# Gate and up on the centred h, with the layer norm's scale multiplied in as their rows leave PSUM

## The chip, the cores and the metric

One core of a Trainium2 chip. The metric is device time in microseconds (us) of one execution. Besides the time, each run lists the span that the profile sees of each execution and the mean clock granted to TensorE over it (1.0 is full). All comparisons are of runs of state fast, the mark for a run within 1.5% of its kernel's fastest.

In the profile's lines PE is TensorE (PEld its weight loads), DVE is VectorE, ACT is ScalarE, DMA a transfer. A load is whole, or has landed, when the last of its 16 semaphore increments is recorded. An eviction is the copy of a product out of PSUM, where the matmuls leave it. The chain of waits is the work that ended last, followed back from its end.

## The reference, cut to what matters

Decode step of one block: layer norm, attention over a cache, layer norm, gated feed-forward, two batch rows.

```python
def _layernorm(x, axis=-1, eps=1e-5):
    m = jnp.mean(x, axis=axis, keepdims=True)
    v = jnp.var(x, axis=axis, keepdims=True)
    return (x - m) / jnp.sqrt(v + eps)
# ... attention A, D = 640, F = 1536, B = 2
def _B_ref(x, w_gate, w_up, w_down):
    return (_gelu(x @ w_gate) * (x @ w_up)) @ w_down
h = x + _A_ref(_layernorm(x, axis=-1), A_k_cache, A_v_cache, A_wq, A_wo)
h2 = h + _B_ref(_layernorm(h, axis=-1), B_w_gate, B_w_up, B_w_down)
```

The scale 1/sqrt(v + eps) is one number per batch row, so it may be multiplied in after the gate and up products, ahead of the gelu.

## The kernel before

The program records operations per engine in order; `R`, `W`, `X` name what an operation reads, writes, and which PSUM bank it uses, and waits follow from them. The tail of the kernel, with cuts marked:

```python
# loads, in this order at the end of one queue: ... wo(2), wo(3), gate, up in 2 parts, down in 4 parts
WDC = ((0, 6), (6, 9), (9, 11), (11, 12))
# ...
def layernorm(src, src_toks, banks, dst, dst_tok, total=None):
    # ... total None: as for x
    else:
        pe(total, R=["rs", "bsel"], X=["m2"])
    dve(lambda e: e.tensor_copy(mean[:, :], m2[:, 16:18]), W=["mean"], X=["m2"])
    dve(tt(dT[:, 0, :, :], src, mean..., ALU.subtract), ...)
    dve(tt(dT[:, 1, :, :], dT[:, 0, :, :], dT[:, 0, :, :], ALU.mult), ...)
    dve(lambda e: e.tensor_reduce(out=ls[:, 1, :], in_=dT[:, 1, :, :]..., op=ALU.add), ...)
    pe(lambda e: e.matmul(m2[:, 20:22], lhsT=onesd[:, :], rhs=ls[:, 1, :], start=True, stop=True), ...)
    act(... ACT.Ln, bias=eps ...); act(... ACT.Exp, scale=-0.5 ...)
    dve(tt(dst, dT[:, 0] ..., lt[:, 1, :] ..., ALU.mult), R=["dT0", "lt1"], W=[dst_tok])
# ...
oproj(3)                        # the last attention weights; h and its row sums
h_columns()                     # h by columns, 20 small fp32 matmuls
layernorm(...)                  # writes hnT, bf16
ffn_in(sps, "s", "wg", ...)     # gate: 20 matmuls, hnT stationary, 384 columns moving
dve(lambda e: e.tensor_copy(grow[0:98, 0:384], sps[0:98, 0:384]), W=["sm"], X=["s"])
# ... transposes of the gate rows, gelu on VectorE and ScalarE
ffn_in(ops_, "o", "wu", WUC)    # up: 20 matmuls in two parts
act(... urow[0:98, :], in_=ops_[0:98, 0:384], func=ACT.Copy ...)
# ... transposes of the up rows, product uT
for i, (f0, f1) in enumerate(WDC):   # down: 48 matmuls, each part waits for its own load
    wd, wtoks = where["wd", i]
    # ...
dve(... yrow <- m1 ...); out is stored
```

## Time and profile before

| | before |
|---|---|
| time, 3 runs | 293.97, 294.00, 294.27 us |
| the profiled execution | 294.86 us, span 292.8, mean clock 0.827 |
| read from HBM | 122.29 MB |

### The profile page before, as it was taken

What the parts mean: (1) busy time and instruction counts of PE and PEld (TensorE: products, weight loads), DVE (VectorE), ACT (ScalarE), POOL (GpSimd) and SP (SyncE); (2) the same over time, 40 slices, a digit from 0 to 9 for tenths busy, and PEclk for the clock granted to TensorE, in tenths of its full rate; (3) what the DMA queues carried; (4) which work ended last, traced back from release to release, by engine and by line L of the source; (5) the groups of instructions that cost most, each with busy time, mean ns of one, the idle gap of its engine ahead of it and who ended that gap; (6) DMA issues with size and microseconds to landing.
All of it is one profiled execution on the core that took longest, in us unless ns stands there. A gap on an engine that the chain in (4) does not pass through costs nothing.

```text
span 292.8 us, 5063 instructions
## 1 busy us (share of the span) xinstructions
PE 197.3 (67%) x2141; PEld 153.7 (52%) x2141; DVE 128.3 (44%) x310; ACT 96.2 (33%) x120; POOL 8.6 (3%) x36
## 2 busy tenths in 40 slices
PE   2450869848677298849495697668696869676575
PEld 1440436718475295628282675366666666653342
DVE  5950075713447055526255255316365425352222
ACT  2150116623442143616152245234343434430000
POOL 4000020000000000000000000000000000000000
PEclk9995679995979579988879599959797969797655
DMA  7998999999999999999999999999999999999993
GB/s 272 468 488 358 435 426 437 432 425 430 425 419 436 430 430 428 430 430 430 433 421 437 430 430 430 430 430 430 430 430 430 433 430 430 430 430 433 419 410 126
DMA packets 6363, 122.44 MB, mean 418 GB/s; under 512 B 719, under 2 KB 849, under 8 KB 1361
## 3 DMA queue, kind: packets, MB, share of 16 engines
q1 hardware_dynamic: 6336, 122.29, 97.8%
q8 instruction: 7, 0.11, 0.2%
q14 instruction: 4, 0.02, 0.0%
q10 hardware_dynamic: 16, 0.01, 0.0%
HBM read 122.29 MB, written 0.00 MB: 418 GB/s over the span
## 4 chain that ended last, share of the span: by engine, by line
DMA 71%; PE 24%; SPq 1%; DVE 1%; issue 1%; ACT 0%
DMA ring<-in_A_k_cache_dram 52%; PE tps L553 16%; DMA ring<-in_A_wq_dram 10%; DMA ring<-in_A_wo_dram 9%; PE tps L574 2%; SPq L343 1%; PE m L706 1%; PE ops L655 1%; PE m L829 1%; PE sps L783 1%; PE ops L783 1%; PE m L688 1%; PE tps L792 1%; PE m L725 0%; DVE ering L404 0%
## 5 line engine op out<-in xcount | busy, mean ns | idle before, releaser
L553 PE MATMUL tps<-identf,ring 128*128 128x128 f32 x768 | 115.6, 319 | 43.7 <-DMA ring<-in_A_k_cache_dram 42.3
L553 PEld LDWEIGHTS tps<-identf,ring 128*128 128x128 f32 x768 | 106.8, 168 | 46.8 <-DMA ring<-in_A_k_cache_dram 43.9
L562 ACT ACTIVATE ktr<-tps 128x1024 bf16<-128x1024 bf16 x80 | 79.4, 1023 | 83.5 <-PE tps L553 83.5
L565 DVE COPY ktr<-tps 128x1024 bf16<-128x1024 bf16 x112 | 74.1, 688 | 70.6 <-PE tps L553 69.8
L630 ACT ACTIVATE eexp<-sm,nm 128x512 bf16<-128x512 f32 x16 | 11.5, 722 | 64.5 <-DVE nm L628 64.5
L655 PE MATMUL ops<-ring,ering 128*32 128x384 bf16 x512 | 24.6, 336 | 4.9 <-DMA ring<-in_A_v_cache_dram 4.8
L611 PE MATMUL sps<-ktr,rq 128*16 128x512 bf16 x384 | 26.0, 405 | 1.1 <-POOL rq L404 1.1
L619 DVE CUSTOM_DVE_ANT_1 sm<-sps,mska 128x512 f32<-128x512 f32 x16 | 11.1, 692 | 35.2 <-PE sps L611 35.2
L655 PEld LDWEIGHTS ops<-ring,ering 128*32 128x32 bf16 x512 | 12.6, 98 | 13.3 <-DMA ring<-in_A_v_cache_dram 6.2
L611 PEld LDWEIGHTS sps<-ktr,rq 128*16 128x16 bf16 x384 | 9.5, 90 | 12.0 <-issue 2.1
L626 PEld LDWEIGHTS m<-mrhs,pm 128*128 128x128 bf16 x16 | 1.5, 96 | 22.9 <-DVE mrhs L400 22.9
L574 PE MATMUL tps<-ring,xnT 128*32 128x384 bf16 x80 | 5.8, 478 | 10.8 <-DMA ring<-in_A_wq_dram 10.8
L626 PE MATMUL m<-mrhs,pm 128*128 128x16 bf16 x16 | 2.9, 183 | 14.7 <-DVE mrhs L400 14.7
L404 POOL TENSOR_TENSOR rq<-qs,mask 128x96 bf16<-128x96 bf16 x16 | 5.6, 359 | 195.3 <-PE sps L611 161.3
L574 PEld LDWEIGHTS tps<-ring,xnT 128*32 128x32 bf16 x80 | 3.3, 138 | 13.2 <-issue 11.0
L597 DVE CAST qs<-ops 128x384 bf16<-128x384 f32 x1 | 0.6, 558 | 17.6 <-PE ops L592 17.6
L404 DVE TENSOR_TENSOR ering<-m,mask 128x256 bf16<-128x256 f32 x16 | 6.7, 420 | 3.4 <-PE m L639 3.4
L458 ACT ACTIVATE lt<-m,eps_t 128x2 f32<-128x2 f32 x2 | 0.5, 262 | 21.2 <-PE m L456 21.2
L706 PE MATMUL m<-ring,ot 128*2 128x320 bf16 x96 | 4.7, 340 | 2.4 <-DMA ring<-in_A_wo_dram 2.4
L581 ACT ACTIVATE qrow<-tps 128x768 bf16<-128x768 f32 x1 | 0.8, 810 | 15.6 <-PE tps L574 15.6
L639 PE MATMUL m<-sel,eexp 128*128 128x64 bf16 x64 | 5.0, 206 | 1.2 <-ACT eexp L630 1.2
L639 PEld LDWEIGHTS m<-sel,eexp 128*128 128x128 bf16 x64 | 4.8, 112 | 1.7 <-DVE nm L628 1.3
(116 smaller groups left out, 88.5 us busy)
## 6 DMA issues: line engine op xcount, KB each, us to landing
ring<-in_A_k_cache_dram SPq DMA_DIRECT2D x16, 3072.0 KB, 31.4
ring<-in_A_v_cache_dram SPq DMA_DIRECT2D x16, 3072.0 KB, 27.3
ring<-in_A_wq_dram SPq DMA_DIRECT2D x1, 7680.0 KB, 28.1
ring<-in_A_wo_dram SPq DMA_DIRECT2D x4, 1920.0 KB, 21.3
ring<-in_B_w_gate_dram SPq DMA_DIRECT2D x1, 1920.0 KB, 31.4
ring<-in_B_w_up_dram SPq DMA_DIRECT2D x1, 1536.0 KB, 24.7
ring<-in_B_w_down_dram SPq DMA_DIRECT2D x1, 960.0 KB, 27.2
ring<-in_B_w_down_dram SPq DMA_DIRECT2D x1, 480.0 KB, 27.9
```

The costliest lines, as they stand in the source:

```text
L404: return lambda e: e.tensor_tensor(out=out, in0=a, in1=b, op=op)
L553: ins = e.transpose(tps[bi][:, 128 * u:128 * (u + 1)], kv[:, off:off + 128], identf[:, :])
L562: act(lambda e, dst=dst, bv=bv: e.activation(out=dst, in_=bv, func=ACT.Copy), W=[("kt", n)], X=[("t", bi)])
L565: dve(lambda e, dst=dst, bv=bv: e.tensor_copy(dst, bv), W=[("kt", n)], X=[("t", bi)], cls=0)
L574: ins = e.matmul(tps[0][32 * r:32 * (r + 1), 0:384], lhsT=xnT[:, c, 32 * J:32 * (J + 1)], rhs=wq[:, c, 1536 * J + 384 * r:1536 * J + 384 * ...
L611: ins = e.matmul(sps[32 * ch:32 * ch + 16, :], lhsT=rq[:, g % 4, k, :], rhs=ktr[:, k // 2, 1024 * ch + k % 2:1024 * (ch + 1):2], start=(k ...
L619: dve(lambda e: e.tensor_tensor_reduce(out=sm[:, :].rearrange("p (u x) -> p u x", u=4), in0=sps[:, :].rearrange("p (u x) -> p u x", u=4), ...
L630: act(lambda e: e.activation(out=eexp[:, :], in_=sm[:, :], func=ACT.Exp, bias=nm[:, 0:1], scale=1.0, accum_out=zr[:, g % 4:g % 4 + 1]), R= ...
L639: ins = e.matmul(o, lhsT=eexp[:, 128 * u:128 * (u + 1)], rhs=sel64[:, :], start=True, stop=True)
L655: ins = e.matmul(ops_[32 * r:32 * (r + 1), 0:384], lhsT=ering[:, g % 4, t, :], rhs=vv[:, 384 * t:384 * (t + 1)], start=(g % 4 == 0 and t < 4),
L706: ins = e.matmul(m1[32 * r:32 * r + 2, 192:512], lhsT=ot[:, kk, :], rhs=wo[:, kk - k0, 320 * h:320 * (h + 1)], start=(kk == 1 or J < 2 and ...
L783: ins = e.matmul(bank[32 * r:32 * r + 2, 0:384], lhsT=hnT[:, c, :], rhs=cols[:, :, 3 * (r % 2):3 * (r % 2) + 3], start=(c == 0), stop=(c = ...
```

## The change

Its intent: take the norm's serial steps off the path between h and the gate. Four parts: the mean's matmul goes ahead of the column matmuls, into a bank of its own; gate and up take the centred h; square, sum, Ln and Exp run beside the gate, with the sum's matmul after eight of its 20; the scale is applied by the two evictions.

```diff
+        dve(lambda e: e.memset(lsx[:, :, :], 0.0), W=["lsx"])
 ...
+        pe(lambda e: e.matmul(tps[3][:, 0:2], lhsT=rs[0:98, :].to_broadcast([98, 128]), rhs=bsel[0:98, :], start=True, stop=True),
+           R=["rs", "bsel"], X=[("t", 3)])
         h_columns()
-        layernorm(m2[:, 32:42].rearrange("p (c b) -> p c b", b=B), [], ["m2"], hnT[:, :, :].unsqueeze(2), "hnT", ...)
+        dve(lambda e: e.tensor_copy(mean[:, :], tps[3][:, 0:2]), W=["mean"], X=[("t", 3)])
+        dve(tt(hnT[:, :, :], hc, mb, ALU.subtract), R=["mean"], W=["hnT"], X=["m2"])
+        dve(tt(dT[:, 0, :, :], hc, mb, ALU.subtract), R=["mean"], W=["dT0"], X=["m2"])
+        dve(tt(dsq[:, :, :, :], db, db, ALU.mult), R=["dT0"], W=["dsq"])
+        dve(lambda e: e.tensor_reduce(out=lsx[:, :, 0:B], in_=dsq[:, :, :, :], axis=AX.X, op=ALU.add), ...)
+        def row_scale():
+            pe(... matmul(tps[2][0:98, 0:1], lhsT=lsx ... [:, 0:98], rhs=onesd[:, 0:1] ...))
+            act(... lnv, ACT.Ln, bias=eps ...)
+            act(... rstd, ACT.Exp, scale=-0.5 ...)
 ...
-        ffn_in(sps, "s", "wg", ((0, NC5),))
-        dve(lambda e: e.tensor_copy(grow[0:98, 0:384], sps[0:98, 0:384]), W=["sm"], X=["s"])
+        ffn_in(sps, "s", "wg", ((0, 2),), ((0, NC5),))
+        row_scale()
+        ffn_in(sps, "s", "wg", ((2, NC5),), ((0, NC5),))
+        dve(ts(grow[0:98, 0:384], sps[0:98, 0:384], rstd[0:98, 0:1], ALU.mult), R=["rstd"], W=["sm"], X=["s"])
 ...
-        act(... func=ACT.Copy), W=[("osb", 0), ("osb", 1)], X=["o"])
+        act(... func=ACT.Identity, scale=rstd[0:98, 0:1]), R=["rstd"], W=[("osb", 0), ("osb", 1)], X=["o"])
```

The rewritten loop of `ffn_in` lets one load be used in two pieces.

## The prediction

> **What bounds the kernel now.** I read the page's rows over time first, for what the whole span is bound by, then the chain of waits, for its last piece, then the DMA issues, for when the last weights land.
>
> ```profile
> DMA  7998999999999999999999999999999999999993
> GB/s 272 468 488 358 435 426 437 432 425 430 425 419 436 430 430 428 430 430 430 433 421 437 430 430 430 430 430 430 430 430 430 433 430 430 430 430 433 419 410 126
> PEclk9995679995979579988879599959797969797655
> DMA 71%; PE 24%; SPq 1%; DVE 1%; issue 1%; ACT 0%
> ```
>
> The transfers are busy in every slice but the last, at 420 to 437 GB/s: 122.29 MB have to come in, and the change removes no byte. So only the end, after the stream has nearly run out, can get shorter. The chain from 275 us on is compute:
>
> ```profile
> 248.00 27.34 DMA ring<-in_A_wo_dram
> ...
> 277.85 1.30 PE m L725 x20
> 279.15 0.53 PE m L773 x2
> 279.68 0.02 issue
> 279.70 0.17 DVE mean L450
> ...
> 281.68 0.18 DVE hnT L404
> 281.86 0.04 issue
> 281.90 1.80 PE sps L783 x19
> 283.70 0.02 issue
> 283.72 0.57 DVE sm L808
> ...
> 288.46 1.81 PE m L829 x48
> 290.27 0.02 issue
> 290.29 0.33 DVE yrow L835
> ```
>
> Columns: start, duration, what. The last attention weights land at 275.34; then h, its columns (L725), the mean (L773), the layer norm, gate (first L783), its eviction (L808), up, down (L829), copy out. Between the mean's matmul (ends 279.68) and the gate (starts 281.90) lie 2.22 us of small serial steps.
>
> The trap is that the chain names only what released each step last. The same transfers still run beside it. The DMA issues, with the start of each issue, say when each weight is whole:
>
> ```profile
> ring<-in_B_w_gate_dram SPq DMA_DIRECT2D x1, 1920.0 KB, 31.4
> ring<-in_B_w_up_dram SPq DMA_DIRECT2D x1, 1536.0 KB, 24.7
> ring<-in_B_w_down_dram SPq DMA_DIRECT2D x1, 160.0 KB, 28.2
> ```
>
> Gate is issued at 248.47 and takes 31.4 us: whole at 279.87. The landing records give wu0 283.57, wu1 284.54, and the four down parts 286.88, 288.07, 288.86, 289.26. Against use: gate at 281.90 (2.03 us to spare), up at 285.10 (1.53 to spare), the first down part at 288.46 (1.58 to spare), but the last part, four matmuls that start at about 289.84 (290.27, less 0.34 for one matmul, less three spacings of 0.03), has only 0.58 us to spare. The busy share of the DMA engines agrees: 0.43 in 288.0 to 288.5, 0.13 in 288.5 to 289.0, then nothing. From 275.34 to 289.26 they bring gate, up and down, 5.90 MB, which is 424 GB/s: the stream is full and can't come sooner.
>
> **What the Trainium skill says.** "DMA: Bandwidth & Descriptors", section "Why a DMA increments its semaphore by 16 and not by 1": only the full count means that everything has landed. The trace agrees: of the last down part the first of 16 increments comes at 287.36 and the last at 289.26, so the late one counts. "TensorE: Matmul & The Clock Gate", Part 1: the tensor clock is full or half, by how busy TensorE was in windows of about 3.4 us. The trace has 0.50 in every window from 275 us on, so the tail's durations are those of the half clock; I keep them. "ScalarE: Activation LUTs", section "What ACT_TABLE_LOAD costs": each per-partition pointer operand adds about 93 ns to an ACTIVATE, and a switch of table set costs about 2.66 us. The changed program has the same single table load as the old one, at its start, so only the 93 ns count; no row of this trace shows them for this shape. "VectorE: DVE Perf Modes", section "Why PSUM operands drop a tier": an fp32 source in PSUM runs at the base rate whatever the operation, so the scaling eviction should last what the plain copy did (0.56 us for 384 columns).
>
> **The change part by part, on the clock of the trace of before.**
>
> 1. The mean's matmul (0.53 to 0.58) goes ahead of the column matmuls (1.30). TensorE is free at about 279.70 as before, but the mean's copy (0.17) now lies beside the column matmuls.
> 2. VectorE then makes the centred h in bf16: 279.70 to 279.88. Gone from between are copy, square, reduction, sum matmul (0.60), Ln (0.27), Exp (0.21) and the final multiply. The gate could start at 279.92. But its weights are whole only at 279.87, and a wait for a transfer is followed in this trace by 0.13 us (275.34 to 275.47) until TensorE starts. So 280.00: 1.90 sooner than 281.90.
> 3. Row scale. VectorE: centred fp32 (0.17), square of 40 columns and reduction of 40 (about 0.2 each, from 0.17 for 10 and 0.18 for 24 columns): ready at about 280.5. TensorE meets its new matmul after eight of the 20 gate matmuls, at 280.00 + 8 x 0.08 = 280.64, so it doesn't wait. The new fp32 matmul (two passes, 128x98 weights) is of the kind of the sum matmul removed, whose weight loads last 0.50 and whose matmuls 0.59; I charge 0.5 us, now inside the gate. Gate ends at 280.00 + 1.80 + 0.5 = 282.3. Ln and Exp (0.5 together) end at about 281.8, beside it.
> 4. Eviction with scale, 0.57: 282.9. Transposes 0.77 and gaps: 283.7. Up weights (283.57 + 0.13) are just there. Up 1.73: 285.45, its last part (284.54) in time.
> 5. Up's eviction on ScalarE 0.50 + 0.09, transposes 0.77, product 0.23, gaps 0.1: down can start at about 287.15, 1.3 us sooner than 288.46. That is the whole gain of compute: 1.98 of norm, less 0.08 of landing, 0.5 of row scale and 0.09 of ScalarE.
> 6. Down then runs into its own weights. 24 matmuls from 287.15 end at 287.9; 12 from 288.07 + 0.13 end at 288.6; 8 from 288.86 + 0.13 at 289.25; the last 4 from 289.26 + 0.13 = 289.39. Four matmuls at a spacing of 0.03 with 0.34 for the last end at 289.82. The copy out starts at 289.84 and not at 290.29: **0.45 us saved**. Of 1.3 us of compute, 0.85 turn into waits for the last down parts.
>
> At the start there is one more small memset on VectorE (lsx), before 13.3 us, delaying copies of the first keys slightly; those are done at 19.9 and the next work waits for the query weights, whole at 29.50, so it costs nothing. Sum: 294.0 - 0.45 = 293.55 us.
>
> **The rivals.**
>
> A. The landings don't bind, and all of the compute gain shows: 294.0 - 1.3 = 292.7. For it: the chain of waits of before has no transfer in it after 275.34. Against: the landing of the last part at 289.26 doesn't depend on compute, since its buffers were free and it was issued by 261.1; and it is 1.0 us before the old end of down.
>
> B. The row scale holds the gate up: VectorE's sums come late, or the fp32 matmul between two groups of gate matmuls drains the pipeline, at 1 us or more and not 0.5. Down has 0.87 us of slack (it may start at 289.39 - 44 x 0.031 = 288.0 without harm), so this costs nothing up to about 1.4 us in all; at 2 us the time would be back to about 294.1. Against it: the sum is ready about 0.15 us before TensorE comes to it.
>
> C. Gate or up wait longer for their own weights, since both are now consumed within about 0.15 us of landing. The landings are fixed by the stream, so this could eat tenths of the compute gain, all of it within the 0.87 us that down waits anyway: 293.55 again.
>
> D. The clock of the last windows changes with the denser work. At full clock the tail's matmuls halve, but they are hidden behind the landings except the last four and the first after 275.34: 0.2 us less, 293.3.
>
> **Range and chances.** The most that could be saved in any way I can see is about 2.2 us (0.7%), and a loss of 2% would take 5.9 us, over twice the whole of the norm. So within 2% it is: 0.985. The three runs of before lie 0.3 us apart, and the landing of the last part moves by tenths between executions; with A at about one in ten and B or a full cancelling at one in ten, the range is 293.0 to 294.0.
>
> **What would show it.** Right: in the profile after, gate starts about 280 with hnT as its releaser or the gate weights; the new matmul sits among the gate matmuls at about 0.5 us; down starts near 287.1 and is spread over about 2.7 us where it took 1.81, with TensorE's waits before it put down to the down weights; the chain of waits ends in the transfer of the down weights, then a few matmuls, then the copy at 1 us or less after 289.26. DMA rows unchanged. Wrong: down in one block of 1.8 us that ends before 289.3 (rival A, landings earlier than I read them), or a gate group that ends after 283.0 (B), or a landing of the last down part that moved by more than 0.3 us, which would mean that the change touches the stream after all.

## The result, and the profile after

The changed kernel took 294.07 us (median of 6, 293.96 to 294.18), the kernel before 294.20 in the same rounds (median of 6, 293.97 to 294.78): ratio 0.9994, 95% interval 0.9981 to 1.0006. A ratio here is the mean time of one kernel's fast runs over that of the other's of the same rounds, so not quite the ratio of the medians. The prediction, 293.55 within 293.0 to 294.0, is missed by 0.07 us at its upper end and by 0.5 at its centre. What is odd: the trace after looks as forecast.

The timeline of the changed kernel, from the column matmuls to the copy out (start, duration, engine, line, operation, tiles, count; in brackets the idle time before it and what ended it):

```profile
278.59 1.30 PE L727 MATMUL m<-hsel,hrow 98*64 98x2 f32 x20
...
279.94 0.17 DVE L408 TENSOR_TENSOR hnT<-m,mean 128x10 bf16<-128x10 f32 x1 [1.08 <-PE m L727]
...
280.26 0.81 PE L801 MATMUL sps<-ring,hnT 128*2 128x384 bf16 x8 [0.36 <-DVE dT L408]
...
281.00 0.49 PE L786 MATMUL tps<-onesd,lsx 128*98 128x1 f32 x2
...
282.60 0.62 DVE L404 TENSOR_SCALAR sm<-sps,rstd 98x384 f32<-98x384 f32 x1 [1.96 <-PE sps L801]
...
285.79 0.58 ACT L840 ACTIVATE osb<-ops,rstd 98x384 f32<-98x384 f32 x1 [0.63 <-PE ops L801]
...
287.50 1.43 PE L850 MATMUL m<-ring,uT 128*17 128x160 bf16 x36 [0.32 <-DVE uT L408]
...
289.14 0.71 PE L850 MATMUL m<-ring,uT 128*17 128x160 bf16 x12 [0.21 <-DMA ring<-in_B_w_down_dram]
```

The clock is half from 273.54 to the end, as in the trace of before (from 273.43). The gate starts at 280.26 and down at 287.50, where they started at 281.90 and 288.46. Down comes in pieces, with a wait for its own weights. The chain of waits of the changed kernel now ends so:

```profile
260.85 28.24 DMA ring<-in_B_w_down_dram
289.09 0.04 issue
289.14 0.74 PE m L850 x12
289.88 0.02 issue
289.91 0.32 DVE yrow L856
```

The third down part heads it, whole at 289.09; the last was whole at 289.50, and the copy out starts at 289.91, where it was 290.29. The transfers took as long as before (changed kernel, DMA issues), but the stream as a whole is 0.23 us later in this trace: the attention weights land at 275.57, where it was 275.34.

```profile
ring<-in_B_w_gate_dram SPq DMA_DIRECT2D x1, 1920.0 KB, 31.5
...
ring<-in_B_w_down_dram SPq DMA_DIRECT2D x1, 160.0 KB, 28.2
```

So one pair of traces shows what was forecast, and the times don't. Either the trace of before isn't the usual execution, or the stream comes later in the changed kernel and eats the gain: the last landing is 289.50 here, 289.26 before.

### The profile page after: what moved, and what is told of

The parts are those of the page before. It is cut to its first block, busy times and chain, and to the rows that moved or that the text cites. A ratio compares the mean times of both kernels' runs of the same rounds, so it can differ in the third digit from the quotient of the medians.

```text
span 292.4 us, 5066 instructions
## 1 busy us (share of the span) xinstructions
PE 196.2 (67%) x2141; PEld 151.6 (52%) x2141; DVE 128.2 (44%) x311; ACT 96.3 (33%) x120; POOL 8.6 (3%) x36
## 4 chain that ended last, share of the span: by engine, by line
DMA 76%; PE 20%; SPq 2%; DVE 1%; issue 0%
DMA ring<-in_A_k_cache_dram 57%; PE tps L555 15%; DMA ring<-in_A_wq_dram 10%; DMA ring<-in_B_w_down_dram 10%; PE tps L576 2%; SPq L347 2%; PE ops L657 1%; PE m L708 1%; PE m L690 1%; DVE ktr L567 0%; DVE ering L408 0%; PE m L850 0%; PE m L641 0%; PE m L671 0%; DVE yrow L856 0%
## 5 line engine op out<-in xcount | busy, mean ns | idle before, releaser
L555 PE MATMUL tps<-identf,ring 128*128 128x128 f32 x768 | 114.4, 317 | 45.4 <-DMA ring<-in_A_k_cache_dram 44.1
L555 PEld LDWEIGHTS tps<-identf,ring 128*128 128x128 f32 x768 | 105.5, 166 | 48.4 <-DMA ring<-in_A_k_cache_dram 45.4
```

The lines of the kernel that those rows point to most:

```text
L555: ins = e.transpose(tps[bi][:, 128 * u:128 * (u + 1)], kv[:, off:off + 128], identf[:, :])
```

## The experiments

Twelve kernels in three calls, each call on one chip (a different one each time) with its own runs of the kernel before. The medians of those are 294.28 (11 runs), 294.65 (9) and 294.40 (7).

**b1: the kernel before, unchanged.** No edit.

> The kernel before, unchanged: a second trace of it and a null comparison. The first trace of it was of an execution of 294.86 us, 0.7 to 0.9 above its medians (294.0, 294.2), so its tail may not be the usual one. Theory 1 (the usual execution of before has a shorter compute tail, because the tensor clock is full in part of the tail, and it ends on the last landing already): this trace, if its execution is near 294.1, shows down less than 0.3 us after the last landing allows, a last landing near 289.3 to 289.5, and a tail from the last attention weights' landing to the start of the last copy of 14.3 to 14.5 us instead of 14.95. Theory 2 (the stream of after is late by 0.2 us or more, by chance or by the change): the tail here is again 14.9 us at the half clock, the last landing is near 289.0, and the execution is near 294.1. Ratio to itself 1.000 within 0.001 for both.

Measured: 294.40 us median (294.09 to 294.91, 6 runs), ratio to itself 1.0002. The profiled execution lasted 294.11 us. Its chain of waits:

```profile
261.20 28.13 DMA ring<-in_B_w_down_dram
289.33 0.04 issue
289.38 0.28 PE m L829 x4
289.65 0.02 issue
289.68 0.32 DVE yrow L835
```

This is the kernel without the change, and it ends on the last landing, with four matmuls and the copy after it. The copy out starts 14.25 us after the last attention weights (275.43), just under the 14.3 to 14.5 of theory 1, and not 14.95 as in the first trace. The stretches of that first trace (columns: stretch, length, busy time of PE, PEld, DVE, ACT, POOL, granted clock, DMA share, GB/s):

```profile
284.00:286.00 2.00, 1.87 (x23) 0.83 (x23) 1.01 (x5) 0.00 (x0) 0.00 (x0) 0.50 0.99 405
286.00:288.00 2.00, 1.41 (x15) 0.54 (x7) 0.66 (x3) 0.71 (x2) 0.00 (x0) 0.50 0.77 297
288.00:290.00 2.00, 1.69 (x49) 1.45 (x48) 0.22 (x1) 0.00 (x0) 0.00 (x0) 0.50 0.14 52
```

and the same stretches of b1, the same program:

```profile
284.00:286.00 2.00, 1.87 (x27) 0.81 (x23) 1.04 (x5) 0.00 (x0) 0.00 (x0) 0.56 1.00 408
286.00:288.00 2.00, 1.18 (x15) 0.49 (x7) 0.92 (x5) 0.71 (x2) 0.00 (x0) 1.00 0.74 282
288.00:290.00 2.00, 1.37 (x48) 0.81 (x48) 0.35 (x2) 0.00 (x0) 0.00 (x0) 1.00 0.12 45
```

The clock column is the difference: 0.50 to the end in one, 1.00 from 285.76 in the other. At the full clock up's end, its transposes and down pass quickly enough that compute is done when the weights are. Over all 33 executions of before in the experiments for which span and clock are listed (b1 among them) there are two levels:

| level of before | executions | span, us | mean clock | time, us |
|---|---|---|---|---|
| lower | 19 | 292.0 to 292.4 | 0.848 to 0.879 | 293.88 to 294.52 |
| upper | 14 | 292.6 to 292.9 | 0.822 to 0.841 | 294.56 to 294.93 |

The mean clock separates them without an overlap. The trace that the prediction was read from (292.8, 0.827) is of the upper one. The second theory falls: the last landing here is 289.33, and the tail isn't 14.9. Whether the lower level as a whole ends on the last landing, as b1 does, b_short tests below.

**a1: the changed kernel, unchanged.** No edit.

> The changed kernel, unchanged, with five rounds. Theory 1: 0.9990 to 0.9998 of before, with a spread of its times half of before's or less, since it ends on the last landing whatever the clock. Theory 2: the last landing of the down weights again 0.2 us or more later than in the traces of before of the same call.

Measured: 293.96 us (293.88 to 294.05, 5 runs), ratio 0.9984 (0.9971 to 0.9997), spans 292.1 to 292.3. The spread is 0.17 us where before had 0.72, as expected; the ratio is lower than expected. Its last landing is 289.28 and the copy out starts at 289.62; this execution had the full clock from 284.43, the first trace of the changed kernel half to the end, with a span of 292.1 against 292.4. In 11 executions of the changed kernel, with mean clocks from 0.823 to 0.873, none goes above 294.18. The stream isn't late by the change.

**b_short and a_short: both kernels without the last three down loads.** The result is wrong; all compute stays.

```diff
-            for i, (f0, f1) in enumerate(WDC):          # the loads
+            for i, (f0, f1) in enumerate(WDC[:1]):
 ...
-            wd, wtoks = where["wd", i]                  # the down product
+            wd, wtoks = where["wd", 0]
```

> Wrong result on purpose: the kernel before without the last three down loads (960 KB); the down product reads the first part's rows again, so all work stays and only the landings of the last 2.3 us of the stream go. The tail is then bound by compute alone. Theory 1: in an execution like the usual one it gains little over before, 0 to 0.3 us, for its own compute ends near there. Theory 2: no gain at all beyond 0.1 us.

Measured: 294.47 us (293.70 to 294.84, 4 runs), ratio 0.9991. Its upper level stays (294.84, 294.71), which shows that level to be bound by compute. The lower level falls: 293.70 here, and 293.38 and 293.22 when the run was repeated below, against 293.88 to 294.52 with all loads. So the landings do hold the lower level, and by more than the 0 to 0.3 us expected.

> Wrong result on purpose: the changed kernel without the last three down loads. If the gain of compute was real and hidden behind the landings, as the prediction has it, it shows here: 0.9 to 1.3 us less than the same shortening of before (a ratio near 0.996 between the two). If the change gains nothing in compute, it is equal to the shortened before within 0.2 us.

Measured: 293.03 us (292.49 to 293.45, 4 runs), ratio 0.9954; to b_short 0.9963 (0.9954 / 0.9991), or 1.1 us. It holds, but both have two levels.

**b_short2 and a_short2: the same two once more.**

> The shortened kernel before once more (wrong result on purpose), as the partner of the other three runs on this chip. Two levels again, near 293.7 with the full clock from 285 us on and near 294.8 without.

> The shortened changed kernel once more (wrong result on purpose). Two levels near 292.5 and 293.45: 1.1 to 1.4 us below the shortened before at the same level. If the levels don't pair like this, the gain of compute read from the first pair was chance.

Measured: b_short2 294.03 us (293.22 to 295.04, 4 runs), a_short2 293.39 (292.27 to 293.48, 4 runs), ratios 1.0000 and 0.9956. Both together: the upper level of shortened before is 294.68, 294.71, 294.84, 295.04, that of the shortened changed kernel 293.33 to 293.48 (five): means 294.82 and 293.43, 1.39 us apart. The lower levels, 293.22, 293.38, 293.70 against 292.27, 292.49, 292.63, are 0.97 apart. One run of shortened before, 294.24, lies between. So the levels pair as expected, the lower ones a little closer than the 1.1 us named. I sorted these runs by their times; here the mean clock does not do it (293.33 has 0.862, 292.27 has 0.853). The traces give it without the spread. Chain of waits of b_short, half clock to the end:

```profile
275.48 0.14 issue
...
282.05 1.80 PE sps L783 x20
...
288.62 1.81 PE m L829 x36
290.43 0.02 issue
290.45 0.33 DVE yrow L835
```

and of a_short2, half clock too:

```profile
275.45 0.14 issue
...
280.14 0.81 PE sps L801 x8
280.95 0.42 PE tps L786 x2
281.37 1.09 PE sps L801 x9
282.46 0.03 issue
282.48 0.63 DVE sm L404
...
287.38 1.81 PE m L850 x48
289.19 0.02 issue
289.21 0.33 DVE yrow L856
```

From the landing to the copy out: 290.45 - 275.48 = 14.97 against 289.21 - 275.45 = 13.76. The change is worth 1.21 us of compute at the half clock. The other two traces have the full clock from 285.85: 289.13 - 275.39 = 13.74 in b_short2 against 288.37 - 275.55 = 12.82 in a_short, so 0.92 there. With the landings in place at most a part of it can be had.

**b_warm and a_warm: dummy matmuls in TensorE's waits ahead of the gate, to keep the clock up.** In before there are 11: the seven of the cut below, two after the mean's matmul and two after the sum's. In the changed kernel there are 8: the same seven and one after the column matmuls.

```diff
+        def warm(n, w=512):
+            for _ in range(n):
+                pe(lambda e: e.matmul(tps[1][:, 0:w], lhsT=identb[:, :], rhs=ktr[:, 0, 0:w], start=True, stop=True), ...)
 ...
         o_columns(3)
+        warm(6)
         oproj(3)
+        warm(1)
```

> The kernel before, with 11 dummy matmuls (128x512, into a PSUM bank that is free then) in TensorE's waits from the last attention output to the gate, so that the tensor clock is full before gate, up and down. Theory 1 (the clock's phase decides whether before ends on compute or on the last landing): the executions of 294.7 to 294.9 are gone, all lie within 0.2 us near 294.1, the last landing heads the end of the chain, ratio to before about 0.999. Theory 2 (the two levels of before have another cause, such as the stream): both levels stay, 3 to 4 in 10 at 294.8.

Measured: 294.23 us (294.07 to 294.36, 5 runs); before had five of nine at 294.65 to 294.87. All five spans are 292.1 to 292.2: the upper level is gone, with no change to the norm. (Five executions alone are few: if 19 in 33 fall into the lower level, five in a row would do so about once in 16 times.) In its trace the clock is full from 269.44 to 279.68 and again from 283.09; the gate starts at 280.97, 0.93 us sooner than in the first trace. Ratio 0.9992, spread 0.29 us where 0.2 was expected. Two lines of its chain of waits:

```profile
261.20 28.14 DMA ring<-in_B_w_down_dram
...
289.68 0.33 DVE yrow L845
```

Which is where b1 and a1 end (289.68, 289.62).

> The changed kernel with 8 such dummy matmuls. Theory 1: equal to the changed kernel and to b_warm within 0.1 us (294.0), for all three end on the same landing. If the change had a gain of its own beside the clock, it would be 0.3 us or more below b_warm.

Measured: 293.98 us (293.91 to 294.05, 5 runs), ratio 0.9981, spans 292.1 to 292.2. It equals the changed kernel, so no version with all its loads beats that one: all end on the last down loads. In its trace the clock was half from 280.92 to the end and the span was still 292.2, so the changed kernel doesn't need the clock. But it is 0.25 us below b_warm, which I had not expected. The spans are equal; the difference lies outside them. Time less span is 1.97 to 2.16 us in the five runs of b_warm and 1.78 to 1.95 in those of a_warm. Over the 33 executions of before its mean is 2.02, over 11 of the changed kernel 1.81. Why a kernel whose profile has three instructions more (5066 against 5063) takes 0.2 us less outside the profiled span I can't say; that stays open.

**b_warm_short and a_warm_short: the same with the last three down loads taken away.** Edits of both kinds above.

> Wrong result on purpose: b_warm without the last three down loads (first part's rows read again). Theory 1, worked out with the full clock: after the last attention weights (275.4) the chain is fast enough that gate and up wait for their own weights (279.9, 284.6) and the first down part (287.0) holds down; copy out near 288.0, time near 292.4 with one level only. Its gate starts near 280.0, so the norm's steps have left the path before the change touches them.

> Wrong result on purpose: a_warm without the last three down loads. Theory 1: equal to b_warm_short within 0.2 us, where a_short gained 1.1 to 1.4 us over b_short at equal clocks: at the full clock the landings of gate, up and the first down part hold both. A rival that holds the change to be worth 1.3 us of compute whatever the clock expects 291.2.

Measured: 293.51 us (292.70 to 293.88, 4 runs) and 293.38 (293.11 to 293.44, 4 runs). They are near each other, but not at 292.4, and not for the reason given: in the trace of b_warm_short the clock is full from 269.08 to 279.32 only and half through gate, up and down, and two dummies sit on the path. Chain of waits of b_warm_short:

```profile
279.64 0.58 PE m L457 x2
280.23 0.88 PE tps L726 x2
281.11 1.73 PE sps L793 x20
```

The 0.88 us of dummies (L726) put the gate at 281.11. In a_warm_short the gate waits for its own weights (280.04). The fastest execution of the pair, 292.70, is one of the kernel before, with a mean clock of 0.887. This pair misses, and whether at a full clock throughout the change would be worth nothing even without the last landings stays untested.

**b_mean_short: one part of the change alone.** On b_short, wrong.

```diff
-                pe(total, R=["rs", "bsel"], X=["m2"])          # in the norm, after h_columns()
+        pe(... matmul(tps[3][:, 0:2], lhsT=rs..., rhs=bsel...), X=[("t", 3)])
         h_columns()
```

> One part of the change alone, on the shortened kernel before (wrong result on purpose): the mean's matmul goes ahead of the column matmuls and its copy lies beside them; the norm is otherwise as before. Expected in its trace: from the start of the mean's matmul to the start of the gate 0.17 to 0.19 us less than the shortened before has from the start of the column matmuls to the gate (4.05 us in its first trace at the half clock). In time 0.2 us at an equal level, which the two levels may hide. A rival, that the reordering also lets the fp32 weight loads overlap, would give 0.4 or more.

Measured: 293.48 us (293.19 to 294.71, 4 runs), levels mixed. Its chain of waits:

```profile
277.38 0.59 PE tps L770 x2
277.97 1.25 PE m L724 x20
...
281.25 1.80 PE sps L784 x20
```

From 277.38 to 281.25 are 3.87 us. In b_short the column matmuls started at 277.99 and the gate at 282.05: 4.06. The part is worth 0.19 us, the length of the mean's copy; the rival of 0.4 falls.

**a_late_short: one part undone, the row scale after the whole gate.** On a_short, wrong.

```diff
-        ffn_in(sps, "s", "wg", ((0, 2),), ((0, NC5),))
-        row_scale()
-        ffn_in(sps, "s", "wg", ((2, NC5),), ((0, NC5),))
+        ffn_in(sps, "s", "wg", ((0, NC5),), ((0, NC5),))
+        row_scale()
```

> One part undone, on the shortened changed kernel (wrong result on purpose): the row scale's matmul comes after all 20 gate matmuls and not after eight. Expected: the gate's matmuls end 0.42 us sooner, but the scale then follows them (0.5 of matmul, 0.5 of Ln and Exp, gaps), so the eviction of gate starts 0.5 to 0.7 us later than with the row scale inside the gate, and the time is 0.5 to 0.7 us more at an equal level. If the matmul inside the gate costs more than it seems there, the eviction would start at the same time or sooner.

Measured: 293.89 us (293.78 to 294.00, 4 runs), all near one level, 0.46 above the upper level of a_short (293.43). Its chain of waits:

```profile
279.97 1.77 PE sps L801 x19
281.74 0.43 PE tps L786 x2
282.18 0.02 issue
282.20 0.27 ACT lnv L788
282.47 0.02 issue
282.49 0.21 ACT rstd L790
...
282.80 0.63 DVE sm L404
```

The eviction starts 2.83 us after the gate, against 2.34 in a_short2 (280.14 to 282.48): 0.49 later, just under the 0.5 to 0.7 expected. The gate's own matmuls last 1.77 us here and 2.32 in a_short2 (280.14 to 282.46), so the matmul in their midst lengthens the gate by 0.55 us and still lets the eviction start 0.49 us sooner.

## Why the prediction was wrong

1. **The forecast tail was right.** Gate 1.9 us sooner by step 2: from the landing of the attention weights to the gate it is 6.56 us before and 4.69 after, 1.87. Row scale 0.5: the gate lasts 2.32 us where it lasted 1.80, 0.52. ScalarE's eviction 0.09 more: 0.58 against 0.49. VectorE's, said to be the same, takes 0.62 against 0.56. Compute gain 1.3: 1.87 less 0.52, 0.09 and 0.06 is 1.20, and 1.21 was measured. Down in pieces, chain ending in the down weights: so it is. Within the pair of half-clock traces the span fell by 0.4 us.

   The wait of step 2 was right as well, though the profile hides it. The line of the gate above names VectorE's dT as what released it. But the gate doesn't read dT, and in a_warm it starts at 280.31, before dT ends at 280.34. In the other six traces of the changed kernel it starts 0.13 or 0.14 us after its own weights are whole (280.12 and 280.26 in the first). So the gate has run into its weights, by 0.1 us (it follows the start of hnT by 0.32 us in the first trace, by 0.22 in a_warm and in before), and a still shorter norm would buy nothing there.

2. **What failed is the sum, "294.0 - 0.45 = 293.55".** It takes a saving read from one execution off the median of others. The trace was of an execution of 294.86 us; of the 33 listed later 14 were like it, and 19 like b1, near 294.2, which ends on the last landing already. From those there is nothing to take by a faster norm. The 11 executions of the changed kernel bear this out. Six have mean clocks of 0.823 to 0.842, like the upper level, and spans of 292.23 on average against 292.77 there: 0.54 saved, near the 0.45 forecast. The other five have 0.847 to 0.873 and 292.20 against the lower level's 292.17: nothing saved. Right would have been: 294.86 less 0.45 is 294.4, and 294.0 stays.

3. **The step behind it is the clock: "The trace has 0.50 in every window from 275 us on, so the tail's durations are those of the half clock; I keep them."** b1 has the full clock from 285.76 with the same program. Its copy starts at 289.68, 0.35 us after the last landing, the changed kernel's (a1) at 289.62, 0.34 after. b_warm removes the upper level without touching the norm; with the two traces of one program above, the clock is shown to be the cause and not only to go with it. The stream is not: the last landing is 289.26 in the upper-level trace and 289.33 in b1. Rival D had named the clock, but put it at 0.2 us and only for the changed kernel; it moves the kernel before by 0.6 (spans of 292.2 and 292.8).

4. **Rival A is settled as argued:** the landings bind, and without them the change is worth 1.0 to 1.4 us (both shortened kernels, level against level). B and C cost what fits into the slack of down, and D was mis-sized as said.

5. **Smaller miss, and some luck:** from the last landing to the copy out I put 0.58 us; it is 0.41 at the half clock and 0.34 at the full one. Of this 0.13 was for TensorE's start after the landing, which took 0.04 (b1: 289.33 to 289.38). In the first trace of the changed kernel the copy out starts at 289.91, close to the 289.84 forecast, because this error and the stream's 0.24 us of delay (last landing 289.50, not 289.26) nearly cancel.

How large the gain is thus depends on how often before falls into its upper level: the ratio was 0.9994 with one run of six near 294.8, and 0.9984 with four of eleven above 294.7. Of the second, some 0.2 us lie outside the span and are not explained.

## What to carry to other kernels

Before taking a saving off the median, compare the profiled execution's own time with the median: if they differ by as much as the saving, the trace is of another state, and a second trace costs little. When the weights land just behind the compute that needs them, a shorter compute chain buys only the distance to the last landing, and what it really buys is steadiness: the changed kernel has 0.3 us between its extremes in 11 executions, the one before 1.05 in 33. A chain of waits that shows no transfer at the end says that none was last in that execution, not that none is close behind.

## What the Trainium skill lacked or had wrong

- "TensorE: Matmul & The Clock Gate", Part 1, has the window free-running and puts the cost of the warm-up under 1% of a typical span. Both fit: the clock changes of a trace lie on one grid of 3.41 us, whose offset from the start of the span is 0.36 us in the first trace of before and 2.46 in b1, and the two levels lie 0.6 of 292 us apart, 0.2%. It says that one kernel's count of slow matmuls varies with the phase; it lacks that the whole time can split into two levels, here 19 and 14 of 33 executions. In the four traces of before and its shortened form, offsets of 0.36 and 0.54 us went with the half clock to the end, 2.46 and 2.54 with the full one from 285.8. It also lacks how busy a window must be: one of 3.41 us with TensorE busy 3.21 us was followed by the full clock (a1), one with 3.22 by the half (the first trace of the changed kernel).
- "VectorE: DVE Perf Modes" lacks a figure for a per-partition scalar on an fp32 source in PSUM: the scaled eviction of 98x384 took 0.62 us, the plain copy 0.56.
- No page says how far apart the 16 increments of one load come at the end of a long stream: in the first trace of before nine of the last down part's came by 287.98 and the other seven from 288.89 to 289.26; in that of the changed kernel fifteen came by 289.05 and the last at 289.50.
